# Token mixing with its tiles loaded into weight buffers, two batches in turn

## The chip, the cores and the metric

The kernel runs on one core of one Trainium2 chip. Its time is the device time in microseconds; three runs of the kernel before took 991.98 us (median), 991.78 and 993.13.

The core's engines each work through a queue of their own, in order: TensorE (PE in the rows, its weight loads PEld), VectorE (DVE), ScalarE (ACT), GpSimd (POOL) and SyncE (SP), which here only issues loads and stores. They wait for one another by semaphores.

## What is computed

Attention over 4 batches of 576 tokens and 8 heads, then two blocks over x of shape 4 x 576 x 512:

```python
def _moe_ref(x, w_ch1, w_ch2):                     # Fourier mixing and the first MLP
   X = np.fft.fft(np.fft.fft(x, axis=1), axis=2)
   u = x + np.real(X)
   un = (u - mu) / np.sqrt(var + 1e-06)            # mean and variance of a token
   return u + np.maximum(un @ w_ch1, 0.0) @ w_ch2  # 512 -> 2048 -> 512

def _moe2_ref(x, w_tok1, w_tok2, w_ch1, w_ch2):
   xt = x.transpose(0, 2, 1)
   h = np.maximum(xt @ w_tok1, 0.0) @ w_tok2       # token mixing: 576 -> 256 -> 576
   u = x + h.transpose(0, 2, 1)
   h2 = np.maximum(u @ w_ch1, 0.0) @ w_ch2         # second MLP: 512 -> 1536 -> 512
   return u + h2
```

## The kernel before

**Split numbers.** Every operand of these products is kept as a high and a low part (`hh` and `hl`, `ch` and `cl`, `uth` and `utl`, weights `..h` and `..l`), and each product is made three times: high by high, high by low, low by high. The weights of the block come in as doubles. `convert` (L73 to L85) loads 512 KB of them into `wraw` (three buffers), makes float32 of them in `wu` (two buffers), and takes the two parts: L78 on ScalarE, L80 on GpSimd, L81 to L83 on VectorE, L84 (high part) on ScalarE, L85 (low part) on GpSimd.

**Weight slots.** Four pools of 16 slots of 128 x 512 hold the weights: `wa`, `wx`, `wb` and `wc`. The first MLP's 16 steps f use four slots each (two matrices, two parts): f 0 to 3 in `wa`, 4 to 7 in `wx`, 8 to 11 in `wb`, 12 to 15 in `wc`. As its last chunk of tokens passes the steps, the slots come free, and `load_wb` fills them, one conversion a call: six for the token mixing (`wt1` and `wt2`, into `wa`), twelve `w1b` and twelve `w2b` of the second MLP. `w1b` go into `wa`, then `wx`, then `wb`; `w2b` into `wb` and, the last six, into the slots of `wa` that held `wt`.

**The MLPs.** The tokens stand in 18 tiles of 128, three tiles to a chunk, six chunks. In a step f of a chunk, `gemm1` makes 12 products of 384 columns (L346), ScalarE takes the relu as `hh` (L350), VectorE the rest `hl` (L351), and `gemm2` makes nine products of 512 columns (L364) into three accumulators that run over all f. The first MLP stores its result in `x2d`; the second takes its tiles from `u2d` (`u_load`), transposes them (L332, L335, L336), and stores the output.

**Token mixing.** Batch b has five tiles, the fifth with 64 rows. `c_load` loads them from `x2d` and splits them (high part on ScalarE, L566; low part on VectorE, L567). `c1(b)` makes 30 products (L614) into two accumulators, with the relu on ScalarE (L619) and its rest on VectorE (L620). `c2(b)` makes 30 more (L629), k over the two halves of the hidden tokens; VectorE adds each to the tile (L636), and SP stores it in `u2d` (L637). Even batches lie in buffers of the first MLP (`u`, `uth`, `utl`), odd ones in the pool `tok`, five buffers of each kind, which opens when `wc` is closed behind the first MLP. Batch 0's first three tiles are loaded in the last chunk of the first MLP, at f = 2; the rest behind it:

```python
        c_load(0, range(3, 5)); c_load(1, range(5)); load_wb()
        for b in range(B):
            hs = c1(b)
            load_wb()
            if b == 3:
                for i in range(2): m2.transposes(0, i, m2.u[0, i])
            c2(b, hs)
            if b + 2 < B: c_load(b + 2, range(5))
            if b == 2:
                for i in range(3): u_load(i)
            load_wb()
        m2.transposes(0, 2, m2.u[0, 2])
```

**What sets the order.** The code gives a program order, and a scheduler of the framework places the instructions of each engine in a queue from it; the slots of a pool are given out when the scheduler finds them free. Which instruction stands behind which is therefore read from the built program, below.

Of the kernel before, what the change touches and what calls it, by code (L numbers as in the profile page):

```python
# [18 lines left out]
DM = 512  # L19
P = 128  # L20
# [21 lines left out]
def attention_fourier_mlp_kernel(ctx: ExitStack, tc: tile.TileContext, a: dict, out: bass.AP):  # L42
# [28 lines left out]

# [1 line left out]
    def convert(src, hi, lo, n, eng):  # L73
# [18 lines left out]

# [1 line left out]
    lt = [(0, t) for t in range(6)]  # L94
# [121 lines left out]

# [1 line left out]
    class Fourier:  # L218
# [91 lines left out]

# [1 line left out]
    def spans(T):  # L312
# [90 lines left out]
    if True:  # L403
# [92 lines left out]

# [1 line left out]
        dp = dst.enter_context(tc.tile_pool(name="mlp", bufs=1, side="right", reuse_waits="tile"))  # L498
# [20 lines left out]
        def load_wb():  # L519
            engine[0] = nc.gpsimd  # L520
            if len(wt) < 12:
                nm, i = "12"[len(wt) // 6], len(wt) % 6 // 2
                src = a["wt" + nm]
                n = min(512, src.shape[1] // 2 - 512 * i)
                wt["h" + nm, i], wt["l" + nm, i] = slot_w(src[:, 1024 * i:1024 * i + 2 * n], wa, "wa", "wt", n)
            elif len(w1b) < NF2:
                f = len(w1b)
                pool, tag = (wa, "wa") if f < 2 else (wx, "wx") if f < 10 else (wb, "wb")
                w1b.append(slot_w(a["w1b"][f], pool, tag, "w1b"))
            elif len(w2b) < NF2:  # L530
                f = len(w2b)
                pool, tag = (wb, "wb") if f < 6 else (wa, "wa")
                w2b.append(slot_w(a["w2b"][f], pool, tag, "w2b"))
# [17 lines left out]
        def c_load(b, ts):  # L551
            for t in ts:
                p, j, (q0, n) = btiles(b)[t]
                if b % 2:
                    r = cp.tile([P, DM], F32, tag="cr", name="cr", bufs=5)
                    h = cp.tile([P, DM], F32R, tag="ch", name="ch", bufs=5)
                    l = cp.tile([P, DM], F32R, tag="cl", name="cl", bufs=5)
                else:
                    r = m1.u_tile(0)
                    if t % 3 == 0:  # L560
                        for nm in ("uth", "utl"):
                            xbuf[nm] = dp.tile([P, 3, DM], F32R, tag=nm, name=nm, bufs=2)
                    h, l = xbuf["uth"][:, t % 3], xbuf["utl"][:, t % 3]
                q = slice(q0, q0 + n)
                nc.sync.dma_start(out=r[q], in_=x2d[p][j, q, :])
                nc.scalar.activation(out=h[q], in_=r[q], func=AF.Copy)  # L566
                nc.vector.tensor_tensor(out=l[q], in0=r[q], in1=f32(h[q]), op=ALU.subtract)  # L567
                xs[b][t] = r, h, l
# [19 lines left out]
        def extra1(c, f):  # L588
            load_wa()
            if c == NCH - 1:  # L590
                if f >= 1:
                    load_wb()
                if f == 2:
                    c_load(0, range(3))

        steps = [(c, f) for h in range(len(PARTS) - 1) for c in range(2) for f in range(PARTS[h], PARTS[h + 1])]
        steps += [(c, f) for c in range(2, NCH) for f in range(NF1)]
        run(m1, steps, prep1, fin1, extra1)
        wcst.close()

# [1 line left out]
        cst = ExitStack()  # L602
        cp = cst.enter_context(tc.tile_pool(name="tok", bufs=1, side="left", reuse_waits="tile"))
        def c1(b):
# [11 lines left out]
            for m in range(2):  # L616
                hh = dp.tile([P, DM], F32R, tag="hh", name="hh", bufs=3)
                hl = dp.tile([P, DM], F32R, tag="hl", name="hl", bufs=3)
                nc.scalar.activation(out=hh, in_=hp[m], func=AF.Relu)  # L619
# [5 lines left out]
        def c2(b, hs):  # L625
# [6 lines left out]
            def fin(t, o):  # L632
# [3 lines left out]
                nc.vector.tensor_tensor(out=r[q], in0=o[q], in1=r[q], op=ALU.add)  # L636
                nc.sync.dma_start(out=u2d[p][j, q, :], in_=r[q])  # L637

# [19 lines left out]
        c_load(0, range(3, 5))  # L658
        c_load(1, range(5))
        load_wb()  # L660
        for b in range(B):
            hs = c1(b)
            load_wb()
            if b == 3:
                for i in range(2):
                    m2.transposes(0, i, m2.u[0, i])
            c2(b, hs)
            if b + 2 < B:
                c_load(b + 2, range(5))
            if b == 2:  # L670
                for i in range(3):
                    u_load(i)
            load_wb()
        m2.transposes(0, 2, m2.u[0, 2])
        cst.close()

# [1 line left out]
        def fin2(T, u):  # L678
# [16 lines left out]

        run(m2, [(c, f) for c in range(NCH) for f in range(NF2)], prep2, fin2, extra2)
        wbst.close()
        dst.close()


# [1 line left out]
PERM = np.concatenate([np.arange(288), np.arange(575, 287, -1)])  # L702
# [3 lines left out]

# [1 line left out]
def _split(x):  # L708
# [86 lines left out]
```

## Time and profile before

| | before |
|---|---|
| median of three runs | 991.98 us |
| span of the profiled execution, first to last instruction | 987.2 us |
| its end-to-end time | not given apart from the span |
| TensorE busy, share of the span | 949.3 us, 96% |
| VectorE busy | 472.8 us, 48% |
| ScalarE busy | 299.9 us, 30% |
| GpSimd busy | 236.1 us, 24% |
| share of the 16 DMA engines taken by SP's queue | 29.3% |
| moved by DMA | 93.00 MB |
| token mixing, first to last product of L614 and L629 | 595.2 to 676.6 us |
| its products, 120 of L614 and 120 of L629 | one of 512 columns: 0.39 to 0.40 us |

The span is on one clock for all engines. A product's own duration overlaps the next one's, so from one product to the next less time passes than the duration of one. The idle time that the profile gives for TensorE is therefore a little less than what is lost.

### The profile page before, as it was taken

The page shows a single profiled execution, that of the slowest core. Times are in us where ns is not written, and L with a number is a line of the kernel's source. Part 1 is how long each engine was busy: PE and PEld are TensorE (multiplying, and loading weights), DVE is VectorE, ACT ScalarE, POOL GpSimd, SP SyncE. Part 2 cuts the span into 40 slices and gives each one's busy share as a digit, 9 for nine tenths or more (in the row PEclk, how much of TensorE's full clock was granted, in tenths as well). Part 3 has the DMA queues.
Part 4 walks back from the last instruction along what each step waited for, and adds up shares of the span by engine and source line. Part 5 has one row for each costly group of instructions (what it writes and reads, how often), then busy time and mean ns, then how long its engine had stood idle before and what let it go on. Part 6 is the DMA issues. An engine that isn't in the chain of part 4 may idle for free.

```text
span 987.2 us, 13400 instructions
## 1 busy us (share of the span) xinstructions
PE 949.3 (96%) x5176; PEld 839.6 (85%) x5176; DVE 472.8 (48%) x895; ACT 299.9 (30%) x821; POOL 236.1 (24%) x187
## 2 busy tenths in 40 slices
PE   6988999999999999999999997989999999999998
PEld 6878888787889988999999995758998889998986
DVE  4679778999983412222123667884121212121211
ACT  5778664333431111111113334442111111111110
POOL 3466456443340000000002775643000000000000
PEclk9889999999999999999999998999999999999999
DMA  9997644243442100100102335682010201000100
GB/s 252 277 298 237 196 147 138 79 134 129 140 127 85 65 1 1 64 1 33 33 1 70 123 112 170 202 265 94 1 65 1 64 1 64 1 33 1 33 1 33
DMA packets 47215, 93.00 MB, mean 94 GB/s; under 512 B 5314, under 2 KB 15656, under 8 KB 47152
## 3 DMA queue, kind: packets, MB, share of 16 engines
q1 hardware_dynamic: 45184, 89.43, 29.3%
q0 software_dynamic: 1968, 2.72, 1.1%
q8 instruction: 41, 0.67, 0.3%
q14 instruction: 22, 0.18, 0.0%
HBM read 68.53 MB, written 23.60 MB: 93 GB/s over the span
## 4 chain that ended last, share of the span: by engine, by line
PE 62%; DVE 17%; DMA 9%; POOL 4%; issue 3%; ACT 3%; SPq 1%; DVEq 0%; POOLq 0%; ACTq 0%
PE oo L364 28%; PE h L346 28%; DVE wu L82 4%; DVE wu L83 3%; DMA xd<-x 2%; POOL wu L80 2%; DVE wu L81 2%; DMA cr<-x2d 1%; ACT sm L167 1%; PE ut L332 1%; DMA vs<-in_vs_dram 1%; PE av L190 1%; PE sc L149 1%; DVE xa L305 1%; DMA u<-ud 1%
## 5 line engine op out<-in xcount | busy, mean ns | idle before, releaser
L351 DVE SCALAR_TENSOR_TENSOR hl<-h,hh 128x384 fp32r<-128x384 f32 x168 | 93.0, 555 | 380.3 <-ACT hh L350 380.3
L350 ACT ACTIVATE hh<-h 128x384 fp32r<-128x384 f32 x168 | 81.9, 489 | 424.1 <-PE h L346 424.0
L346 PE MATMUL h<-uth,wAh 128*128 128x384 f32 x384 | 130.2, 340 | 0.0
L346 PE MATMUL h<-uth,wAl 128*128 128x384 f32 x384 | 129.6, 338 | 0.0
L346 PE MATMUL h<-utl,wAh 128*128 128x384 f32 x384 | 129.5, 337 | 0.0
L364 PE MATMUL oo<-wAh,hh 128*128 128x512 f32 x288 | 114.0, 398 | 1.5 <-DVE utl L336 0.9
L364 PE MATMUL oo<-wAl,hh 128*128 128x512 f32 x288 | 113.6, 394 | 0.0
L364 PE MATMUL oo<-wAh,hl 128*128 128x512 f32 x288 | 106.0, 395 | 2.4 <-DVE hl L351 2.4
L346 PE MATMUL h<-uth,w1bh 128*128 128x384 f32 x288 | 97.6, 340 | 0.0
L346 PE MATMUL h<-uth,w1bl 128*128 128x384 f32 x288 | 96.7, 336 | 0.0
L346 PE MATMUL h<-utl,w1bh 128*128 128x384 f32 x288 | 96.7, 336 | 0.0
L364 PE MATMUL oo<-w2bh,hh 128*128 128x512 f32 x216 | 86.1, 399 | 0.0
L364 PE MATMUL oo<-w2bl,hh 128*128 128x512 f32 x216 | 85.6, 396 | 0.0
L80 POOL TENSOR_SCALAR wu<-wu 128x512 f32<-128x512 f32 (+1 forms) x38 | 74.3, 1962 | 27.9 <-ACT wu L78 26.8
L364 PE MATMUL oo<-w2bh,hl 128*128 128x512 f32 x216 | 80.1, 394 | 0.0
L346 PEld LDWEIGHTS h<-uth,wAl 128*128 128x128 f32 x384 | 72.1, 188 | 3.2
L346 PEld LDWEIGHTS h<-utl,wAh 128*128 128x128 f32 x384 | 72.2, 188 | 2.5
L346 PEld LDWEIGHTS h<-uth,wAh 128*128 128x128 f32 x384 | 72.1, 188 | 1.9 <-issue 0.2
L167 ACT ACTIVATE sm<-sc,st 96x128 f32<-96x128 f32 (+2 forms) x176 | 61.4, 368 | 28.7 <-DVE st L165 22.4
L364 PEld LDWEIGHTS oo<-wAh,hl 128*128 128x128 f32 x288 | 53.9, 188 | 15.8 <-DVE hl L351 3.3
L85 POOL TENSOR_TENSOR wtl<-wu,wth 128x512 fp32r<-128x512 f32 (+1 forms) x6 | 6.9, 1149 | 242.3 <-ACT wth L84 242.3
L364 PEld LDWEIGHTS oo<-wAh,hh 128*128 128x128 f32 x288 | 54.1, 188 | 12.3 <-DVE u L368 1.4
(148 smaller groups left out, 1700.8 us busy)
## 6 DMA issues: line engine op xcount, KB each, us to landing
wraw<-in_w1a_dram SPq DMA_DIRECT2D x16, 512.0 KB
wraw<-in_w2a_dram SPq DMA_DIRECT2D x16, 512.0 KB
wraw<-in_w1b_dram SPq DMA_DIRECT2D x12, 512.0 KB
wraw<-in_w2b_dram SPq DMA_DIRECT2D x12, 512.0 KB
qz<-in_qt_dram SPq DMA_DIRECT2D x14, 288.0 KB
k<-in_kt_dram SPq DMA_DIRECT2D x7, 576.0 KB
vl<-in_vl_dram SPq DMA_DIRECT2D x4, 768.0 KB
x2d<-u SPq DMA_DIRECT2D x12, 256.0 KB
```

Of the source, the lines that this page charges most:

```text
L80: eng.tensor_scalar(f32(u), f32(u), E_MIN, E_MAX, op0=ALU.max, op1=ALU.min)
L81: v.tensor_scalar(u, u, 4, 1, op0=ALU.logical_shift_left, op1=ALU.logical_shift_right)
L82: v.scalar_tensor_tensor(out=u, in0=high, scalar=-2**31, in1=u, op0=ALU.bitwise_and, op1=ALU.bitwise_or)
L83: v.scalar_tensor_tensor(out=u, in0=low, scalar=29, in1=u, op0=ALU.logical_shift_right, op1=ALU.bitwise_or)
L149: nc.tensor.matmul(out=sc[:q, j * k:(j + 1) * k], lhsT=qz[self.g][:, hp, e, qs], rhs=k_t[self.b, self.g][:, hp, ks], start=False, stop=j = ...
L167: nc.scalar.activation(out=smv[:, j, :], in_=sc[:, j, :], func=AF.Exp, scale=SCALE, bias=st[:, 1, j:j + 1], accum_out=st[:, 2, j:j + 1])
L190: nc.tensor.matmul(out=self.o[:q, (2 * j + e) * 64:(2 * j + e + 1) * 64], lhsT=self.pt[e][:k, j * q:(j + 1) * q], rhs=v[:k, kv(t) if self. ...
L305: nc.vector.tensor_tensor(out=x[:n, 0:257], in0=x[:n, 0:257], in1=m[:n, 0:257], op=ALU.add)
L346: nc.tensor.matmul(out=h[:, :384], lhsT=l[:, ws], rhs=r[:, kd, :], start=x == 0, stop=x == 11)
L350: nc.scalar.activation(out=hh, in_=h[:, :384], func=AF.Relu)
L351: nc.vector.scalar_tensor_tensor(out=hl, in0=h[:, :384], scalar=0.0, in1=f32(hh), op0=ALU.max, op1=ALU.subtract)
L364: nc.tensor.matmul(out=self.o[c][i], lhsT=l[:, s], rhs=r, start=first and x == 0, stop=last and x == 2)
```

## The change

Batches 1 to 3 get slots of the weight pools: 1 and 3 in `wx`, 2 in `wc`; batch 0 stays where it was. The pool `tok` goes, and `wc` stays open to the end. Batch 1 is loaded in the last chunk of the first MLP at f = 9, batch 2 behind it, batch 3 after `c2(1)`. The second MLP's weights move to other pools accordingly. The products go as c1(0), c1(1), c2(0), c2(1), c1(2), c1(3), the transposes of the second MLP's first chunk, c2(2), c2(3). For this an odd batch's relu goes into `uth` and `utl` instead of `hh` and `hl`. The first three tiles of batch 0 are no longer stored in `u2d` and loaded again: the second MLP takes them where they lie.

```diff
-                pool, tag = (wa, "wa") if f < 2 else (wx, "wx") if f < 10 else (wb, "wb")
+                pool, tag = (wa, "wa") if f < 2 else (wb, "wb") if f < 10 else (wc, "wc")
                 w1b.append(slot_w(a["w1b"][f], pool, tag, "w1b"))
...
-                pool, tag = (wb, "wb") if f < 6 else (wa, "wa")
+                pool, tag = (wa, "wa") if f < 6 else (wc, "wc") if f < 9 else (wx, "wx")
                 w2b.append(slot_w(a["w2b"][f], pool, tag, "w2b"))
...
-                if b % 2:
-                    r = cp.tile([P, DM], F32, tag="cr", name="cr", bufs=5)
-                    h = cp.tile([P, DM], F32R, tag="ch", name="ch", bufs=5)
-                    l = cp.tile([P, DM], F32R, tag="cl", name="cl", bufs=5)
+                if b:
+                    pool, tag = (wc, "wc") if b == 2 else (wx, "wx")
+                    r = pool.tile([P, DM], F32, tag=tag, name="cr")
+                    h = pool.tile([P, DM], F32R, tag=tag, name="ch")
+                    l = pool.tile([P, DM], F32R, tag=tag, name="cl")
...
                 if f == 2:
                     c_load(0, range(3))
+                if f == 9:
+                    c_load(1, range(5))
...
-        wcst.close()
...
-        cst = ExitStack()
-        cp = cst.enter_context(tc.tile_pool(name="tok", bufs=1, side="left", reuse_waits="tile"))
         def c1(b):
...
-                hh = dp.tile([P, DM], F32R, tag="hh", name="hh", bufs=3)
-                hl = dp.tile([P, DM], F32R, tag="hl", name="hl", bufs=3)
+                if b % 2:
+                    if m == 0:
+                        th, tl = (dp.tile([P, 3, DM], F32R, tag=nm, name=nm, bufs=2) for nm in ("uth", "utl"))
+                    hh, hl = th[:, m], tl[:, m]
+                else:
+                    hh = dp.tile([P, DM], F32R, tag="hh", name="hh", bufs=3)
+                    hl = dp.tile([P, DM], F32R, tag="hl", name="hl", bufs=3)
...
-                nc.sync.dma_start(out=u2d[p][j, q, :], in_=r[q])
+                if b == 0 and t < 3:
+                    m2.u[0, t] = r
+                else:
+                    nc.sync.dma_start(out=u2d[p][j, q, :], in_=r[q])
...
-        c_load(1, range(5))
+        c_load(2, range(5))
+        hs = [c1(0), c1(1)]
         load_wb()
-        for b in range(B):
-            hs = c1(b)
+        for b in range(2):
+            c2(b, hs[b])
             load_wb()
...
+        c_load(3, range(5))
+        for b in range(2, 4):
+            hs.append(c1(b))
             load_wb()
-        m2.transposes(0, 2, m2.u[0, 2])
...
+        for i in range(3):
+            m2.transposes(0, i, m2.u[0, i])
+        for b in range(2, 4):
+            c2(b, hs[b])
+            for _ in range(2):
+                load_wb()
```

Three places in the queues show what the scheduler makes of it. The first is SP's queue around the end of the first MLP. `wraw` are raw weights, `x2d<-v` the stores of the first MLP's last three tiles, `cr<-x2d` loads of a batch of 1 to 3. Before, with batch 1's five loads among and behind those stores:

```order
L75 DMA wraw<-in_w1b_dram 128x1024 x12
L75 DMA wraw<-in_w2b_dram 128x1024 x3
L571 DMA x2d_78<-v 128x512
L565 DMA cr<-x2d_77 128x512
L571 DMA x2d_78<-v 128x512 x2
L565 DMA cr<-x2d_77 128x512 x3
L565 DMA cr<-x2d_77 64x512
```

Of the change, where batch 1's loads (`x2d_77`) stand a little further ahead among the `w1b`; these are the last of them, with batch 3's first, batch 2's five, and then the stores:

```order
L566 DMA cr<-x2d_77 64x512
L566 DMA cr<-x2d_78 128x512
L75 DMA wraw<-in_w1b_dram 128x1024 x4
L566 DMA cr<-x2d_78 128x512
L75 DMA wraw<-in_w1b_dram 128x1024
L566 DMA cr<-x2d_78 128x512
L75 DMA wraw<-in_w1b_dram 128x1024
L566 DMA cr<-x2d_78 128x512
L75 DMA wraw<-in_w2b_dram 128x1024
L566 DMA cr<-x2d_78 128x512
L566 DMA cr<-x2d_78 64x512
L75 DMA wraw<-in_w2b_dram 128x1024
```

Ten loads have moved ahead of the stores of the first MLP's last tiles.

The second place is TensorE's queue at the end of c1(0): `tk_5823` and `tk_5824` are its accumulators before, `hh_5855` its first relu, `tu` the accumulators of c2(0), `ch_5782` batch 1's first tile.

```order
L614 MATMUL tk_5824<-uth_5772,wth_5284 128x512
L614 MATMUL tk_5824<-utl_5773,wth_5284 128x512
L614 MATMUL tk_5824<-uth_5772,wtl_5285 128x512
L629 MATMUL tu_5875<-hh_5855,wth_5322 128x512
L629 MATMUL tu_5876<-hh_5855,wth_5322 128x512
L629 MATMUL tu_5877<-hh_5855,wth_5322 128x512
L614 MATMUL tk_5956<-ch_5782,wth_5194 128x512
```

Of the change, with `tk_5877` and `tk_5878` for c1(1) and `hh_5869` for the first relu of c1(0); fifteen products on `tk_5877` stand between c1(0) and the first of c2(0), and these are the last of them, with what follows:

```order
L614 MATMUL tk_5877<-cl_5544,wth_5232 128x512
L614 MATMUL tk_5877<-ch_5543,wtl_5233 128x512
L614 MATMUL tk_5877<-ch_5549,wth_5284 128x512
L614 MATMUL tk_5877<-cl_5550,wth_5284 128x512
L614 MATMUL tk_5877<-ch_5549,wtl_5285 128x512
L634 MATMUL tu_5927<-hh_5869,wth_5322 128x512
L634 MATMUL tu_5928<-hh_5869,wth_5322 128x512
L634 MATMUL tu_5929<-hh_5869,wth_5322 128x512
L614 MATMUL tk_5878<-ch_5525,wth_5194 128x512
```

Half of c1(1) has moved ahead of c2(0).

The third place is VectorE's queue at c2(2), whose additions are the rows of L636 before and of L641 now. Before, the five additions of batch 2 with the low parts of batch 3 among them:

```order
L636 TENSOR_TENSOR u_5920<-tu_6147,u_5920 128x512
L83 SCALAR_TENSOR_TENSOR wu_6405<-wraw_6403,wu_6405 128x512
L636 TENSOR_TENSOR u_5926<-tu_6148,u_5926 128x512
L636 TENSOR_TENSOR u_5930<-tu_6149,u_5930 128x512
L567 TENSOR_TENSOR cl_6073<-cr_6071,ch_6072 128x512
L567 TENSOR_TENSOR cl_6079<-cr_6077,ch_6078 64x512
L636 TENSOR_TENSOR u_5934<-tu_6174,u_5934 128x512
```

Of the change, from the last low part of batch 3 on; `wu_6242` is the third of `w2b`, `uth_6170` the second MLP's first chunk, `cr_5807` batch 2's first tile:

```order
L568 TENSOR_TENSOR cl_6064<-cr_6062,ch_6063 64x512
L641 TENSOR_TENSOR cr_5548<-tu_6017,cr_5548 64x512
L625 SCALAR_TENSOR_TENSOR utl_6153<-tk_6120,uth_6152 128x512
L336 TENSOR_TENSOR utl_6171<-ut_6172,uth_6170 128x4x128
L625 SCALAR_TENSOR_TENSOR utl_6153<-tk_6121,uth_6152 128x512
L81 TENSOR_SCALAR wu_6242<-wu_6242 128x512
L336 TENSOR_TENSOR utl_6171<-ut_6179,uth_6170 128x4x128
L82 SCALAR_TENSOR_TENSOR wu_6242<-wraw_6240,wu_6242 128x512
L641 TENSOR_TENSOR cr_5807<-tu_6193,cr_5807 128x512
L641 TENSOR_TENSOR cr_5813<-tu_6194,cr_5813 128x512
```

Batch 3's low parts have moved ahead of c2(2), and in their place two steps of a conversion stand in front of its first addition.

## Rows read from the trace of the kernel before

**Rows 1.** Windows: busy us of PE, PEld, DVE, ACT, POOL; PEclk, DMA share, GB/s.

```profile
610.00:620.00 10.00, 6.48 (x21) 5.21 (x22) 8.17 (x12) 4.72 (x8) 3.81 (x3) 0.66 0.57 203
660.00:670.00 10.00, 7.54 (x29) 5.22 (x29) 5.85 (x8) 4.68 (x8) 6.92 (x5) 0.83 0.83 273
```

**Rows 2.** Waits of TensorE from 590 to 700 us.

```profile
PE tk L614 <- ACT ch L566: 5.5, 2, 4.0
PE ut L332 <- DMA u<-u2d: 2.5, 2, 2.2
PE tu L629 <- ACT hh L619: 1.5, 1, 1.5
PE tu L629 <- DVE u L636: 0.5, 1, 0.5
```

**Rows 3.** Timeline of TensorE: start us, duration, product, idle time before it.

```profile
602.18 0.39 PE L364 MATMUL oo<-wAh,hl 128*128 128x512 f32 x1
602.41 0.40 PE L614 MATMUL tk<-utl,wth 128*128 128x512 f32 x1
...
606.72 0.39 PE L614 MATMUL tk<-uth,wtl 64*128 64x512 f32 x1
608.58 0.96 PE L629 MATMUL tu<-hh,wth 128*128 128x512 f32 x3 [1.47 <-ACT hh L619]
613.52 0.79 PE L614 MATMUL tk<-ch,wth 128*128 128x512 f32 x1 [3.98 <-ACT ch L566]
...
617.00 0.86 PE L629 MATMUL tu<-hh,wth 128*128 128x512 f32 x3
...
645.13 0.39 PE L629 MATMUL tu<-hh,wtl 128*128 128x512 f32 x1
647.08 0.73 PE L614 MATMUL tk<-ch,wth 128*128 128x512 f32 x2 [1.57 <-ACT ch L566]
...
661.42 0.39 PE L614 MATMUL tk<-ch,wtl 64*128 64x512 f32 x1
663.99 0.66 PE L332 MATMUL ut<-ident_r,u 128*128 128x128 f32 x4 [2.18 <-DMA u<-u2d]
...
668.20 0.40 PE L629 MATMUL tu<-hh,wtl 128*128 128x512 f32 x1
...
678.42 0.40 PE L364 MATMUL oo<-w2bh,hh 128*128 128x512 f32 x1
```

**Rows 4.** Chain that ended last, 635 to 655 us: start us, us, what.

```profile
639.52 4.06 DMA u2d<-cr
...
645.16 6.39 DMA cr<-x2d
```

**Rows 5.** L567 by its line, and L80 on the page: durations in ns.

```profile
L567 DVE TENSOR_TENSOR utl<-u,uth x10: 674/683/1099, 529.3 to 636.3; 128x512 fp32r<-128x512 f32 x8, 64x512 fp32r<-64x512 f32 x2
L567 DVE TENSOR_TENSOR cl<-cr,ch x10: 677/690/693, 613.5 to 658.4; 128x512 fp32r<-128x512 f32 x8, 64x512 fp32r<-64x512 f32 x2
...
L80 POOL TENSOR_SCALAR wu<-wu 128x512 f32<-128x512 f32 (+1 forms) x38 | 74.3, 1962 | 27.9 <-ACT wu L78 26.8
```

**Rows 6.** Timeline of ScalarE: first and last high part of w2b, two relus.

```profile
616.22 0.61 ACT L84 ACTIVATE w2bh<-wu 128x512 fp32r<-128x512 f32 x1
...
682.46 0.63 ACT L84 ACTIVATE w2bh<-wu 128x512 fp32r<-128x512 f32 x1 [2.70 <-DVE wu L83]
...
686.99 0.49 ACT L350 ACTIVATE hh<-h 128x384 fp32r<-128x384 f32 x1 [3.52 <-PE h L346]
691.23 0.49 ACT L350 ACTIVATE hh<-h 128x384 fp32r<-128x384 f32 x1 [3.75 <-PE h L346]
```

**Rows 7.** Timeline of SP and VectorE in a quiet stretch of the first MLP.

```profile
315.03 1.51 SPq L571 DMA_DIRECT2D x2d<-u  x3
317.10 1.01 SPq L380 DMA_DIRECT2D u<-ud  x2
...
319.75 1.53 DVE L389 BATCH_NORM_STATS2 bs<-u 128x6 f32<-128x512 f32 x2 [1.81 <-DMA u<-ud]
```

More of the change, by code (lines that the diff above doesn't have):

```diff
@@ L658, in attention_fourier_mlp_kernel @@
         c_load(0, range(3, 5))
-        c_load(1, range(5))
+        c_load(2, range(5))
+        hs = [c1(0), c1(1)]
         load_wb()
-        for b in range(B):
-            hs = c1(b)
+        for b in range(2):
+            c2(b, hs[b])
             load_wb()
[L664 to L672, printed above, removed]
-            load_wb()
-        m2.transposes(0, 2, m2.u[0, 2])
-        cst.close()
+        c_load(3, range(5))
+        for b in range(2, 4):
+            hs.append(c1(b))
+            load_wb()
+        for i in range(3):
[4 more added lines that the diff above has]
+                load_wb()
         def fin2(T, u):
@@ L696, in attention_fourier_mlp_kernel @@
         run(m2, [(c, f) for c in range(NCH) for f in range(NF2)], prep2, fin2, extra2)
+        wcst.close()
         wbst.close()
```

## The prediction

> **What bounds the kernel now.** The profile's first two parts and then the windows were read first: TensorE is busy in nearly all of the span (the table above), and the one stretch after the attention in which it is not is the token mixing, some 80 us long. There the windows show 6.48 and 7.54 us of products in ten, and a granted clock of 0.66 and 0.83 on the mean, where 1.00 is the upper of TensorE's two levels (2.4 GHz) and 0.50 the lower (1.2): the lower one for two thirds and one third of those windows [rows 1]. On both sides the products stand end to end, so any time that TensorE gets back here comes off the end of the kernel: the chain of waits from here on is products alone. The view of TensorE's waits for this stretch then says on whom it waits: ScalarE's copies of batch 1's and 3's tiles, twice, 5.5 us; the loads of the second MLP's first tiles, 2.5 us; once on a relu and once on an addition, 2.0 us [rows 2].
>
> The size of each is best read from product to product in the timeline, since the ends of products are modelled. Two neighbours start 0.23 us apart (602.18 and 602.41, where the first MLP ends) [rows 3]. What lies above that [rows 3]:
> - 606.72 to 608.58, c2(0) waits for the relu of c1(0), which it follows directly: 1.86 - 0.23 = 1.63 us.
> - 608.58 to 613.52, three products and then batch 1's first tile: 4.94 - 0.69 = 4.25 us.
> - 613.52 to 617.00, eight products at the lower clock: 3.48 - 1.84 = 1.64 us.
> - 645.13 to 647.08, batch 3's first tile: 1.95 - 0.23 = 1.72 us.
> - an accumulator that VectorE has not emptied: 0.5 us [rows 2].
> - 661.42 to 663.99, the first tiles of the second MLP come back from memory: 2.57 - 0.23 = 2.34 us.
> - 663.99 to 668.20, at the lower clock again: six products (1.38) and eight transposes. A transpose moves a quarter of a product's columns; estimated at 0.09 us, between a quarter and a half of a product's step, they make 0.7. Lost: 4.21 - 1.38 - 0.7 = 2.13 us.
>
> The sum is 14.2 us. That is the most that this stage can give back, but for small change where products of 64 and 128 rows follow each other, which both kernels have.
>
> Why are the tiles late? Batch 1 has buffers of its own in a pool that opens when the last weights of the first MLP are free, and its loads stand in SP's queue behind the store of the first MLP's last tiles. Batch 3 takes batch 1's buffers, so its load waits 4.06 us for a store and then takes 6.39 [rows 4].
>
> **The change, part by part.** *Batch 1 into wx, batch 2 into wc, both while the first MLP still runs.* SP's rows show batch 1's five loads and the first of batch 3 among the w1b loads, batch 2's behind them, all ahead of the store that they stood behind. The 4.25 and, with it, the 1.64 at the lower clock go. The copies and low parts (ten L567 of 0.69 us, 6.9 us in all on VectorE [rows 5]) move from the token mixing under the last ten steps of the first MLP, of 4.24 us each [rows 6]: 0.69 more in a step that TensorE fills with products. I cost that at nothing; if the cover is gone, it costs what the third and fourth rival say. What the weights pay for the slots comes under w2b below.
>
> *Both products over two batches in turn.* TensorE's rows show c1(1) between c1(0) and c2(0), so fifteen products, 3.5 us, stand where TensorE waited 1.63 for the relu: that goes. The number of products, copies, additions and conversions is the same.
>
> *Batch 3 over batch 1's slots.* This wait stays in kind: the low part of its fourth tile stands in VectorE's queue until the store of batch 1's first tile has landed, behind it the addition of batch 1's second tile, whose store lets the load of batch 3's last tile go, and then its copy. Allowed is the time from the last product of batch 1's first tile to the first product on batch 3's last tile: by TensorE's rows 62 products and three transposes, with the row changes between 64 and 128 rows some 15.3 us. Needed, in a quiet time: a store lands in 2.07 us (315.03 to 317.10, where a load waits for it) and a load in 2.65 (317.10 to 319.75, its reader) [rows 7]: 1.7 until the first addition has gone through VectorE, 2.07, 0.69 low part, 0.68 addition, 2.07, 2.65, 0.63 copy: 10.5 us, no wait. In the busiest: 1.7 + 4.06 + 1.37 + 4.06 + 6.39 + 0.63 = 18.2, a wait of 2.9 [rows 4]. Only two raw loads are let go in that time, and both before the second store, so I take the quiet end, 0.
>
> *The conversions of w2b wait longer.* Before, the first w2b was converted at 616.22 [rows 6]; now its slots are those of wt1, and its place in ScalarE's queue is behind batch 3's last copy. Ahead of it GpSimd's queue stands still as well: the eleventh w1b takes slots in wc that batch 2's first tile lets go only in c1(2), some 75 products, 18 us, behind the first MLP. VectorE's rows show where this is felt: L81 and L82 of the third w2b stand ahead of c2(2)'s additions, and the next accumulators of c2 wait for these. Nothing shows the size of that wait in the new order; its kind is there once now with 0.5 us [rows 2]. Below it could be nothing, above it could cost twice the 1.72 of a late tile, 3.4. I take two of the known size, 1.0 us, since two conversion steps stand ahead.
>
> *The second MLP's first tiles stay.* Three stores and three loads of 256 KB go, and the 2.34 and 2.13 us with them: the transposes take tiles that VectorE finished in c2(0), with c2(1), c1(2) and most of c1(3) between.
>
> Sum: 14.2 - 1.0 = 13.2 us. The span is 987.2 us, and the median of the runs is 4.8 above it; the profiled execution's own end-to-end time isn't given apart, so these 4.8 us are taken as what lies around. 991.98 - 13.2 = 978.8 us.
>
> **A rule against it.** The ten L567 now run while GpSimd converts weights. The row: twenty of them took 0.67 to 1.10 us with a median of 0.68 and 0.69 [rows 5], while GpSimd was busy 3.81 and 6.92 us of ten [rows 1]; so they are hardly held up. The Trainium skill (SBUF — State Buffer, Who interferes with whom) says that a VectorE instruction with two SBUF inputs contends with a GpSimd instruction that reads SBUF, and that the later one blocks until the other is through. By that rule each could be held for one GpSimd step, and the sum would be that of the fourth rival.
>
> **Rivals.**
> 1. *The wait moves to batch 3's last tile.* For it: VectorE and SP stand one behind the other through two stores and a load. 2.9 us, and the two gaps above 2 us were each followed by products at the lower clock, so 2.1 more: 983.8 us. Against: the raw loads are through by then.
> 2. *Slower: the second MLP waits for w2b.* Before, nine of twelve were converted when its products began, now about three. The first conversion ends some 0.6 us behind the first product on batch 3's last tile: 602.4 plus 162 products, three transposes and the row changes, 642.5. The twelfth is needed eleven steps behind the first product on w2b: 678.42 - 13.2 [rows 3] + 11 x 4.24 = 711.9. At the pace of before, (682.46 - 616.22) / 11 = 6.02 us [rows 6], it is there at 708.7. From 6.3 us each on, TensorE waits, eleven times the excess; from 7.5 on, the gain is gone, and at 8 the time is 978.8 + 11 x 1.7 = 997.5 us. Against: the 6.02 itself holds waits for slots, which are free sooner now.
> 3. *Relus late in the first MLP.* ScalarE takes them in turn with the copies of batch 1 and 2, which wait for their loads. A slot is let go one step, 4.24 us, ahead of its copy; a load beside raw weights takes 6.39 [rows 4]: 2.15 late, five tiles of batch 2: 10.8. A relu has some products ahead of it, and I have no row for how many microseconds that is: half, 5.4: 984.2 us.
> 4. *VectorE held up by GpSimd.* Ten times one L80 of 1.96 us [rows 5] is 19.6 on VectorE; half of it at TensorE: 988.6 us. Against: the medians.
>
> **Chances and range.** My forecast 0.62, between 977.8 (no new wait) and 981.2 (3.4 us of it); rival 1 0.13, rival 2 0.12, of which 0.03 end near no change, rival 3 0.08, rival 4 0.05. What a measurement here can tell from no change is about 0.2%, 2 us. Faster by more than that: 0.62 + 0.13 + 0.08 + 0.05 = 0.88; the same 0.03; slower 0.09. The range takes in rivals 1 and 3 and leaves 2 and 4 out (0.17): 977.0 to 985.5, its lower end 0.8 below the case without any new wait, for what the sum's steps of 0.23 may be off.
>
> **What would show it.** Right: no wait of TensorE for a copy of cr or for u2d in its first chunk; a granted clock of 1.00 throughout this stage; c2(0) without a gap; short waits on VectorE's additions around c2(2). Wrong: a wait ahead of batch 3's last tile; idle TensorE in the last chunk of the first MLP, with ScalarE waiting for cr; products on w2b that wait for L84 or L85.

## The result, and the profile after

The change took 983.09 us (median of 4 runs, 981.91 to 984.13) against 991.88 before (4 runs, 987.72 to 993.13), a ratio of 0.990 with an interval of 0.986 to 0.994. A second set of runs gave 982.28 (6 runs) against 992.23 (17 runs, 987.41 to 999.17), 0.9895 (0.9856 to 0.9934). The forecast was 978.8, with 977.0 to 985.5 as its range.

The two windows of [rows 1], now of the change:

```profile
610.00:620.00 10.00, 10.00 (x40) 6.63 (x39) 7.96 (x13) 3.52 (x7) 1.53 (x1) 1.00 0.62 189
660.00:670.00 10.00, 10.00 (x49) 8.51 (x48) 7.50 (x13) 2.12 (x4) 3.14 (x3) 1.00 0.86 258
```

TensorE has no idle time there any more, and its clock is the upper one throughout. GpSimd, which converts weights, is busy 1.53 us of ten instead of 3.81; the stage begins 7.5 us later in this trace, and in the first ten us behind the first MLP's last product it is 1.80 instead of 6.94. Keep these numbers in mind. Of TensorE's waits from 520 to 700 us only one is left, and it is not in the token mixing but in the last chunk of the first MLP:

```profile
PE oo L364 <- DVE hl L351: 1.2, 1, 1.2
```

TensorE's timeline shows the stage as [rows 3] did:

```profile
521.13 0.60 PE L332 MATMUL ut<-ident_r,lm 128*128 128x128 f32 x4
...
609.73 0.39 PE L364 MATMUL oo<-wAh,hl 128*128 128x512 f32 x1
609.96 0.39 PE L614 MATMUL tk<-utl,wth 128*128 128x512 f32 x1
...
614.59 0.50 PE L614 MATMUL tk<-ch,wth 128*128 128x512 f32 x1
...
618.48 0.96 PE L634 MATMUL tu<-hh,wth 128*128 128x512 f32 x3
...
650.55 0.73 PE L614 MATMUL tk<-ch,wth 64*128 64x512 f32 x2
...
673.55 0.40 PE L364 MATMUL oo<-w2bh,hh 128*128 128x512 f32 x1
...
975.13 0.84 PE L364 MATMUL oo<-w2bh,hl 128*128 128x512 f32 x3
```

From here on two stretches are compared, each the difference of two such rows. **A** goes from the first MLP's last transposes to its last product, 521.13 to 609.73: the last chunk, 88.60 us. **B** goes from there to the last product of all, 609.73 to 975.13: 365.40 us. Before, with 602.18 from [rows 3] and these two, A is 87.11 and B 981.49 - 602.18 = 379.31.

```profile
515.07 0.60 PE L332 MATMUL ut<-ident_r,lm 128*128 128x128 f32 x4
...
981.49 0.86 PE L364 MATMUL oo<-w2bh,hl 128*128 128x512 f32 x3
```

So B is 13.9 us shorter, and A 1.5 longer. Ahead of A, where both kernels have the same queues, this execution of the change happened to be 6.1 us later (521.13 against 515.07).

### The profile page after: what moved, and what is told of

It reads as the page before. It is cut to its first block, busy times and chain, and to the rows that moved or that the text cites. A ratio compares the mean times of both kernels' runs of the same rounds, so it can differ in the third digit from the quotient of the medians.

```text
span 980.6 us, 13395 instructions
## 1 busy us (share of the span) xinstructions
PE 948.8 (97%) x5176; PEld 840.1 (86%) x5176; DVE 471.6 (48%) x895; ACT 300.0 (31%) x821; POOL 235.6 (24%) x187
## 4 chain that ended last, share of the span: by engine, by line
PE 75%; DVE 13%; DMA 6%; issue 2%; ACT 2%; SPq 1%; POOL 0%; DVEq 0%; POOLq 0%
PE oo L364 32%; PE h L346 31%; PE tk L614 3%; PE tu L634 3%; DMA xd<-x 3%; DVE wu L82 3%; PE sc L149 1%; DVE wu L83 1%; PE av L190 1%; ACT sm L167 1%; PE ut L332 1%; DMA vs<-in_vs_dram 1%; DVE xa L305 1%; DMA u<-ud 1%; DVE u L368 1%
## 5 line engine op out<-in xcount | busy, mean ns | idle before, releaser
L80 POOL TENSOR_SCALAR wu<-wu 128x512 f32<-128x512 f32 (+1 forms) x38 | 74.8, 1975 | 28.5 <-ACT wu L78 24.5
L85 POOL TENSOR_TENSOR wtl<-wu,wth 128x512 fp32r<-128x512 f32 (+1 forms) x6 | 6.8, 1148 | 242.5 <-ACT wth L84 242.5
```

Source lines behind the costliest of these rows:

```text
L80: eng.tensor_scalar(f32(u), f32(u), E_MIN, E_MAX, op0=ALU.max, op1=ALU.min)
```

## The experiments

Twelve kernels were run. The table has the whole of what they showed; below they stand by what they ask.

| run | time, us | ratio to before (interval) | A | B |
|---|---|---|---|---|
| before, its first trace | 991.88 | | 87.11 | 379.31 |
| again_before | 993.09 | 1.0008 (0.9979 to 1.0037) | 87.10 | 378.41 |
| change, its first trace | 983.09 | 0.990 (0.9863 to 0.9938) | 88.60 | 365.40 |
| again_after | 982.28 | 0.9895 (0.9856 to 0.9934) | 88.32 | 365.40 |
| loads_alone | 981.71 | 0.9875 (0.983 to 0.9921) | 87.88 | 365.62 |
| batch1_late | 980.56 | 0.9883 (0.9841 to 0.9925) | 87.11 | 365.52 |
| both_late | 978.69 | 0.9853 (0.9802 to 0.9905) | 87.10 | 363.99 |
| slots_alone | 981.71 | 0.9886 (0.9808 to 0.9964) | 87.10 | 366.49 |
| before_hold | 986.01 | 0.9933 (0.9902 to 0.9964) | 87.11 | 372.74 |
| before_hold2 | 985.41 | 0.9934 (0.9904 to 0.9963) | 87.10 | 369.77 |
| early1_running | 988.32 | 0.9958 (0.993 to 0.9986) | 88.73 | 371.90 |
| early1_held | 984.16 | 0.9894 (0.9844 to 0.9943) | 88.39 | 366.22 |
| rows64_together | 981.42 | 0.9874 (0.9832 to 0.9917) | 88.93 | 364.66 |
| loads_ahead | 983.47 | 0.9897 (0.9857 to 0.9937) | 87.14 | 364.68 |

**again_before, again_after**: the two kernels as they are, for second traces.

> The kernel before, unchanged, for a second trace. The first trace of the change lost 4.0 us against that of before ahead of the first MLP (its first product at 167.88 against 163.86 us), though the queues are the same up to there. If this is a difference from one execution to the next, this trace or its times show it without the change: a first product near 168 us and a span near 990, and several of the runs near 992 us with others near 988. If the change itself slows the attention, the first product stands at 163.9 us again and the times within 0.2% of one another.

> The changed kernel, unchanged. From the first MLP's last product to the eighth step of the second MLP the first traces took 106.1 us before and 92.5 now: 13.6 us less. If the rest of the difference (6.6 us of span instead of 13.6) is variation of the executions ahead of it, the ratio of the times comes to 0.987 to 0.990 over more runs, and the wait of 1.2 us for VectorE's low part in the first MLP's last chunk, behind batch 1's last copy, is there again. If that wait is chance, it is gone in this trace.

The first MLP's first product stood at 168.67 us in this trace of before and at 166.46 in this one of the change, so the 4.0 us ahead of it were not the change's. Its place went from 163.86 to 173.79 us over all the traces, with equal queues up to there. A and B on the other hand repeat better: B was 365.40 in both traces of the change, and 0.9 us apart in those of before. The wait in A was there again (0.90 instead of 1.18 us), so it is no accident. From here on A and B decide, since a difference of 1 us can't be read from the times. Each of the other kernels has one trace.

**loads_alone**: batches 1 to 3 in weight slots, the rest undone.

```diff
-        hs = [c1(0), c1(1)]
...
+        for b in range(4):
+            hs = c1(b)
...
+            if b == 3:
+                for i in range(3):
+                    u_load(i)
+                for i in range(3):
+                    m2.transposes(0, i, m2.u[0, i])
+            c2(b, hs)
...
```

> Batches 1 to 3 in weight slots as in the change, but the products written batch by batch, and the first three tiles stored and loaded again. Theory A, the prediction's sum: the order is worth 1.6 us and the first tiles in place 4.5 (2.34 of wait and 2.13 at the lower clock), so this is 6.1 us slower than the change, 989 us. Theory B, the early tiles do nearly all: with them there the scheduler puts half of c1(1) ahead of c2(0) by itself, and the tiles of the second MLP are loaded in time: within 1.5 us of the change, 982 to 985 us, no wait of TensorE above 0.5 us for a relu or for a load.

B was 365.62 and TensorE waited for nothing from 600 to 700 us. Theory A was wrong: with the tiles in weight slots, the written order and the tiles in place are worth 0.2 us together. The scheduler puts fifteen products of c1(1) ahead of c2(0) by itself, and the three tiles come back from memory in time.

**batch1_late**, then **both_late**: the change, with tiles that can't be early: batch 1, and then batch 2 too, reads the rows of the first MLP's last three tiles, and so waits for their stores. These kernels compute the batch from other tokens, and their output is not the block's; the number of loads, products and slots is the same.

```diff
-                nc.sync.dma_start(out=r[q], in_=x2d[p][j, q, :])
+                src = x2d[1][6 + t % 3, q, :] if b == 1 else x2d[p][j, q, :]
+                nc.sync.dma_start(out=r[q], in_=src)
...
-                if f == 9:
-                    c_load(1, range(5))
...
+        c_load(1, range(5))
         c_load(2, range(5))
```

In both_late the condition is `b in (1, 2)`.

> The change, but batch 1 reads the rows of the first MLP's last three tiles, so that its loads wait for their stores (batch 1 is computed from other tokens); order, slots and the tiles in place stay. Theory A, the early load of batch 1 carries 4.25 + 1.64 us: c2(0) stands behind c1(0) again and waits 1.6 for the relu, c1(1) waits 0 to 4 us for its tiles and the clock falls: 985 to 990 us. Theory B, the two batches in turn hide a late tile: less than 1 us slower than the change.

> The run before with batch 2 made late as well: batches 1 and 2 read the rows of the first MLP's last three tiles (both are computed from other tokens), so no tile but batch 0's is there when the first MLP ends; slots, order and the tiles in place stay as in the change. Theory A, one batch that is there early is what the scheduler fills the stage with: now TensorE waits for copies again, 4 to 8 us in all with the time at the lower clock, and the stretch from the first MLP's last product to the last product, 365.4 us in the change and 365.5 with batch 1 late, grows to 370 to 373. Theory B, it isn't the early load but that the w2b conversions stand still here, which leaves ScalarE, GpSimd and the queues to batch 1 and 2: at most 2 us of waits, 365.5 to 367.5.

B was 365.52 and 363.99, with at most one wait of 0.2 us. So the early load, which the prediction had as the main thing, can be taken away, for one batch and for both, and nothing is lost; A even falls to 87.1, as before the change. That brought up theory B: what matters is that the conversions stand still here.

**before_hold**: the kernel before with the two halves of w2b exchanged, so that the first six wait for `wt`.

```diff
-                pool, tag = (wb, "wb") if f < 6 else (wa, "wa")
+                pool, tag = (wa, "wa") if f < 6 else (wb, "wb")
```

> The kernel before with the two halves of w2b exchanged: the first six take the slots of wt, the last six those of wb, so the conversions stand still through most of the token mixing as they do in the change; loads, order and first tiles are those of before. Theory A (early tiles): the waits for batch 1's and 3's copies and for u2d stay, 8 to 11 us above the products' steps between the first MLP's last product and the first w1b product. Theory B (conversions out of the way): the relu of c1(0) is no longer late (1.6 us gone), and batch 1's loads, without raw weights beside them, land 1 to 2 us earlier: 4 to 6 us left. In both the second MLP's first chunk may wait for w2b, up to 20 us, since the conversions begin only behind c1(3); that part says nothing on this question.

Neither was right as it stood. B fell by 5.7 to 6.6 us, to 372.74, from two numbers in one line. But what went were the later waits (batch 3's copy, u2d and the lower clock behind them); the first two stayed whole, 1.69 and 4.23 us. At that time it was the last two w1b that were converted, not w2b.

**slots_alone**: loads_alone with both batches late, as in both_late. **before_hold2**: the last two w1b are held as well, and w2b behind them, since the conversions go in order; the diff is that of before_hold2.

```diff
-                pool, tag = (wa, "wa") if f < 2 else (wx, "wx") if f < 10 else (wb, "wb")
+                pool, tag = (wx, "wx") if 2 <= f < 10 else (wa, "wa")
...
-                pool, tag = (wb, "wb") if f < 6 else (wa, "wa")
+                pool, tag = (wb, "wb") if f < 8 else (wa, "wa")
```

> The weight slots of the change and nothing else of it: products written batch by batch, the first three tiles through memory, and batches 1 and 2 read the rows of the first MLP's last three tiles (both are computed from other tokens), so that neither is there early. Theory A: two batches in turn and the tiles in place carried the stage while both batches were late; without them the waits for copies and for u2d come back, 5 to 10 us, and the stretch from the first MLP's last product to the last product is 370 to 375 us. Theory B: the slots are what counts, since they hold the conversions back until the third batch is under way: 364 to 366.5 us, at most 2 us of waits.

> The kernel before with the last two w1b in the slots of wt1, so that all conversions from w1b's eleventh on stand still from the end of the first MLP until c1(3) is through; loads, buffers, order and first tiles are those of before. Holding w2b alone removed the later waits of the stage, not the first two (1.69 and 4.23 us and the lower clock behind them). Theory B (conversions in the way of ScalarE's relu and VectorE's last additions of the first MLP, on which the stores and batch 1's loads wait): now these shrink too, to at most 2.5 us together. Theory A (batch 1's own late load, behind the stores in SP's queue): 4 to 6 us of them stay. The second MLP may wait for weights in its first chunk, which is read apart.

Slots alone, with no tile early, no order and nothing in place, gave 366.49: 1.1 us short of the whole change, and 2.5 short of both_late, which has late tiles too, but the order and the tiles in place. The windows of slots_alone show GpSimd without any work at the time at which it was busy before [rows 1]:

```profile
610.00:620.00 10.00, 10.00 (x42) 7.60 (x42) 5.92 (x10) 3.72 (x6) 0.00 (x0) 1.00 0.75 264
620.00:630.00 10.00, 9.57 (x43) 6.38 (x41) 4.52 (x7) 3.16 (x5) 0.00 (x0) 1.00 0.98 320
```

The kernel before with its conversions held came to 369.77. The wait for the relu is gone there, and of the stage's waits one is left:

```profile
PE tk L614 <- ACT ch L566: 2.9, 1, 2.9
```

How the conversions were in the way is read from the timeline of the kernel before, ScalarE's rows at the end of the first MLP:

```profile
605.34 0.63 ACT L84 ACTIVATE w1bh<-wu 128x512 fp32r<-128x512 f32 x1 [2.12 <-DVE wu L83]
605.88 0.66 ACT L78 ACTIVATE wu<-wraw 128x512 f32<-128x512 f32 x1
606.44 0.63 ACT L566 ACTIVATE uth<-u 128x512 fp32r<-128x512 f32 x1
607.37 0.67 ACT L78 ACTIVATE wu<-wraw 128x512 f32<-128x512 f32 x1 [0.30 <-POOL w1bl L85]
607.95 0.57 ACT L619 ACTIVATE hh<-tk 128x512 fp32r<-128x512 f32 x1
612.84 0.63 ACT L566 ACTIVATE ch<-cr 128x512 fp32r<-128x512 f32 x1 [4.31 <-DMA cr<-x2d]
```

The relu at 607.95 stands behind a conversion's L84 that waited 2.12 us for VectorE and an L78 that waited for GpSimd. In slots_alone ScalarE sat idle 7.60 us ahead of the same relu, ready for it:

```profile
601.83 0.68 ACT L78 ACTIVATE wu<-wraw 128x512 f32<-128x512 f32 x1
610.11 0.60 ACT L623 ACTIVATE hh<-tk 128x512 fp32r<-128x512 f32 x1 [7.60 <-PE tk L613]
```

There the relu starts 3.2 us behind the first MLP's last product (606.92); before, 5.8 us behind it (602.18). VectorE's queue had conversions in it as well. Before, L83 stood ahead of the first MLP's last additions (L368), behind whose stores batch 1's loads stand, so that these additions began 3.1 us behind the last product:

```profile
603.65 1.66 DVE L83 SCALAR_TENSOR_TENSOR wu<-wraw,wu 128x512 int32<-128x512 int32 x1
605.23 1.87 DVE L368 TENSOR_TENSOR v<-oo,v 128x512 f32<-128x512 f32 x3
```

In slots_alone the last two began 0.5 us behind it:

```profile
607.39 1.28 DVE L368 TENSOR_TENSOR v<-oo,v 128x512 f32<-128x512 f32 x2
```

Why the conversions stand still is in the slots: the eleventh w1b needs those that batch 2 holds until c1(2), and w2b those of wt1.

Held conversions are not all that the slots do for late batches: with these held in both, before_hold2 is 3.3 us longer than slots_alone. Its trace differs in two things. The last steps of the tenth w1b still stand ahead of L368, which begins 2.1 us behind the last product. And the scheduler puts nine products of c2(0) ahead of batch 1's first one (three before, eighteen in slots_alone), so that this one meets its late copy:

```profile
615.95 0.85 PE L614 MATMUL tk<-ch,wth 128*128 128x512 f32 x2 [2.88 <-ACT ch L566]
```

In slots_alone the copy has come when TensorE gets there:

```profile
616.10 0.86 PE L613 MATMUL tk<-ch,wth 128*128 128x512 f32 x3
```

No run takes these two apart.

**early1_running, early1_held**: does an early batch 1 help when the conversions run on? Batches 1 and 3 go into `wx` in the kernel before, and w1b and w2b where slots are free; in the second, the last two w1b and the last four w2b go into `wa` again.

```diff
-                pool, tag = (wa, "wa") if f < 2 else (wx, "wx") if f < 10 else (wb, "wb")
+                pool, tag = (wa, "wa") if f < 2 else (wb, "wb") if f < 10 else (wc, "wc")
...
-                pool, tag = (wb, "wb") if f < 6 else (wa, "wa")
+                pool, tag = (wc, "wc") if f < 6 else (wa, "wa")
...
-                    r = cp.tile([P, DM], F32, tag="cr", name="cr", bufs=5)
+                    r = wx.tile([P, DM], F32, tag="wx", name="cr")
...
```

> The kernel before, with batches 1 and 3 in slots of wx so that batch 1 comes in under the first MLP; w1b and w2b go to wb and wc, where slots are free, so the conversions run on through the stage as they do before. Batch 2's buffers, the written order and the first tiles are those of before. The stretch from the first MLP's last product to the last product is 378.4 to 379.3 us before, 365.4 in the change, 366.5 with the slots alone and both batches late, 369.8 before with the conversions held. If an early batch 1 is enough by itself, the first two waits go although the conversions run (the scheduler puts half of c1(1) behind c1(0)): 368 to 371 us, the waits for batch 3 and for u2d staying or going with it. If the conversions are what delays this stage, at least 4 us of waits are left in all: 373 to 378 us.

> The run before this, with the last two w1b in the slots of wt1, so that the conversions stand still from the first MLP's end until c1(3) is through, as in the second run on the kernel before. With that one (369.8 us, batch 1 late) and the run before this it makes two by two: batch 1 early or late, conversions running or held. If the two causes add up, this one loses nothing more in the stage: 365.0 to 366.5 us. If one of them is enough, it is within 1 us of the better of the other two.

It does. Early means here the load and the order that the scheduler makes of it, with half of c1(1) ahead of c2(0). B in us, two by two:

| | conversions run on | conversions held |
|---|---|---|
| batch 1 late | 378.4, 379.3 | 369.8 |
| batch 1 early | 371.9 | 366.2 |

Holding is worth 8.6 to 9.5 us with a late batch 1 and 5.7 with an early one; an early load 6.5 to 7.4 and 3.6. Each removes half of the loss or more, and the two together, less than their sum, nearly all of it. The waits that stay when the conversions run on are of the kind that [rows 2] show:

```profile
PE tk L610 <- ACT ch L566: 1.4, 1, 1.4
PE tu L625 <- ACT hh L615: 0.7, 1, 0.7
PE tu L625 <- DVE cr L632: 0.5, 1, 0.5
PE tk L610 <- ACT uth L566: 0.3, 1, 0.3
```

**rows64_together**, then **loads_ahead**: what the change still leaves.

```diff
-            for ts in ((0, 1, 2), (3, 4)):
+            for ts in ((0, 1, 2), (3,), (4,)):
```

The second adds that a tile of batch 1 is allocated and loaded one tile ahead:

```diff
             for t in ts:
...
+                for s in (t, t + 1):
+                    if s in ts and s not in lead and (s == t or b == 1):
+                        load(s)
```

> The change, with the products on 64 rows of both halves of c1 one behind the other. In the change's trace, products about a change between 128 and 64 rows lose 0.09 to 0.11 us each, eight of them in c1(0), 0.82 us. If it is the change of rows that costs this, half of the changes in c1 go, and with four batches the stretch from the first MLP's last product to the last product shrinks from 365.4 to 363.8 to 364.2. If it is something else about these products (their weight loads, the accumulator), it stays within 0.3 us of 365.4.

> The run before this, and batch 1's tiles loaded one tile ahead of their copies' slots. In the change, the copy of batch 1's last tile waits for its load in ScalarE's queue, behind it a conversion's first step, GpSimd's, VectorE's and at last the low part that TensorE waits for: 1.2 and 0.9 us in the two traces of the change, 0.45 in that of the loads alone, none where batch 1 came late. If that chain is the cause, the wait in the first MLP's last chunk goes to below 0.3 us; if the early conversions themselves are too slow for a step of 4.2 us, it stays at 0.4 to 1.2. Time 979 to 981 us against 982.3 for the change, which the spread of the runs may cover.

With the 64-row products of c1(0) side by side, c1(0) took 4.25 us from the first product behind the first MLP to the first of batch 1 (610.32 to 614.57) instead of 4.63 (609.96 to 614.59 in the change). The scheduler let only two of the four batches be written so (seven stretches of 64-row products are left of nine), hence 0.74 us in B instead of 1.2 to 1.6. In loads_ahead the wait in A is gone and A is back at 87.14. This is the best of the kernels that compute the whole: A + B is 451.8 us, against 454.0 and 453.7 in the traces of the change. The times don't show it (983.47): the spread ahead of the first MLP covers it, whose first product stood at 173.79 us in this trace.

## Why the prediction was right, and where not

**The size of the stage's loss: right.** The sum said that 14.2 us could come back and 13.2 would. B gave back 13.0 (378.41 - 365.40) to 13.9.

**Its cause: half of it.** The first step that failed is "*The conversions of w2b wait longer*", which was priced at -1.0 us, with a bound of -3.4. What was seen of it was right (GpSimd's queue stands still until c1(2)), and the sign was wrong: the standstill cleared ScalarE's and VectorE's queues and, in the kernel before, was worth 5.7 us beside an early batch 1 and 9 without. There was no wait for an addition around c2(2). The terms 4.25 and 1.64 were given to batch 1's early load alone. It does take them away, but so do the slots with late loads (slots_alone); held conversions by themselves leave 3.04 and 1.58 of them (before_hold2).

**"I cost that at nothing": wrong.** The copies and low parts under the first MLP cost 1.2 to 1.5 us in A; the chain is told under rival 3. The wait for additions that didn't come had been priced at 1.0, so the two errors nearly cancel in the time: that part of the hit is luck.

**"c2(0) waits for the relu of c1(0), which it follows directly": wrong.** c2(0)'s first products need the relu of c1(0)'s first half only, and six products lie between. The relu was late because ScalarE's queue had conversions in front of it. With these held and the order of before, the wait is gone (before_hold2). So it was no matter of the order, and two batches in turn were worth nothing once the slots and the early tiles were there (loads_alone). With late tiles, order and tiles in place together gave 2.5 us (both_late against slots_alone).

**The first tiles in place, 2.34 + 2.13: not theirs.** before_hold (conversions held) and early1_running (conversions on, batch 1 early) both lost this wait with the tiles still going through memory.

**Batch 3's last tile: right.** Forecast quiet, 10.5 us of 15.3 allowed. Measured the same way it was 12.8 of 16.1: its product came at 650.55 without a wait, 3.3 us after its copy ended.

**w2b for the second MLP: right.** The first high part was written at 647.99 and the last at 703.11, 5.0 us each, and no product on w2b waited. Rival 2 had its point at 7.5 us each.

```profile
647.99 0.64 ACT L84 ACTIVATE w2bh<-wu 128x512 fp32r<-128x512 f32 x1 [0.74 <-PE tk L614]
...
703.11 0.63 ACT L84 ACTIVATE w2bh<-wu 128x512 fp32r<-128x512 f32 x1 [2.54 <-DVE wu L83]
```

**Rival 3 came true beside the forecast**, with 1.2 to 1.5 us of its 5.4. In the change, ScalarE's rows in the last chunk of the first MLP are:

```profile
577.43 0.63 ACT L567 ACTIVATE ch<-cr 64x512 fp32r<-64x512 f32 x1 [4.04 <-DMA cr<-x2d]
578.08 0.68 ACT L78 ACTIVATE wu<-wraw 128x512 f32<-128x512 f32 x1
578.65 0.63 ACT L84 ACTIVATE w1bh<-wu 128x512 fp32r<-128x512 f32 x1
579.18 0.49 ACT L350 ACTIVATE hh<-h 128x384 fp32r<-128x384 f32 x1
```

The relu at 579.18 is in time all the same. What is late is its low part on VectorE: that stands behind L81 of the conversion whose L78 stood behind the waiting copy, with GpSimd's L80 between.

```profile
580.80 1.50 DVE L81 TENSOR_SCALAR wu<-wu 128x512 int32<-128x512 int32 x1 [2.02 <-POOL wu L80]
582.22 0.54 DVE L351 SCALAR_TENSOR_TENSOR hl<-h,hh 128x384 fp32r<-128x384 f32 x1
```

TensorE then goes on at 582.82, having waited 1.18 us. Some 1.07 of this is the 1.50 us of L81 above its median of 0.43, an estimate; the last section has the reason. Late batches (A = 87.10 or 87.11 in seven traces, before's two among them) or a load one tile ahead (87.14, the copy waits 1.28 us instead of 4.04) take it away: this chain is shown.

**The 4.8 us "around" the span were a misreading**, though nothing in the sum hangs on it, which takes 13.2 off the median. The time lies 1.7 to 2.1 us above the span in every run since. So the profiled execution of before, with its span of 987.2, took about 989.0 us: it stood in the lower part of before's runs and was set beside the median of others. The forecast was 3.5 to 4.3 us too low. From A and B the change is worth 12.1 us (the mean of 466.4 and 465.5 less that of 454.0 and 453.7), so 980 from the 992.2 of before; what is measured above that, 2 to 3 us, lies within the spread of the stretch ahead of the first MLP, whose cause stays open.

Not tried: early tiles for batches 1 and 2 while the conversions run on, since the four pools have no place for them: two batches take 30 of the 64 slots, wt 12, and the 22 that are left hold eleven w1b at most.

Why both_late is 1.4 us better than the change in B can be read from its trace. It has six stretches of 64-row products where the change has nine, and in one of them those of batch 1 (rows 64 to 127) and batch 2 (rows 0 to 63) stand side by side. Seven products start there within 0.70 us, 0.12 apart instead of 0.23:

```profile
630.40 0.40 PE L613 MATMUL tk<-cl,wth 64*128 64x512 f32 x1
630.41 0.50 PE L613 MATMUL tk<-ch,wth 64*128 64x512 f32 x1
630.64 0.39 PE L613 MATMUL tk<-ch,wtl 64*128 64x512 f32 x1
630.75 0.51 PE L613 MATMUL tk<-cl,wth 64*128 64x512 f32 x2
630.98 0.51 PE L613 MATMUL tk<-ch,wtl 64*128 64x512 f32 x2
```

Three stretches at 0.37 us (0.74 for two in rows64_together) and 0.7 us here, less 0.3 for its one wait, make 1.5: an estimate, and no run isolates it.

## What to carry to other kernels

A wait names the last releaser; look at what stood in front of that releaser in its own queue before giving the time to an edit. Background work (here weight conversions) in the queues of a short critical stage can cost more than late loads, and a pool's slots decide when it runs: one or two of the lines that choose a pool gave 5.7 to 9.5 us of the stage. Undo each part of a change by itself: of three edits here one carried nearly all of it, in part for a reason that was counted as its price. And compare stretches of the trace that repeat to within 1 us, where the times of whole runs spread by 5 to 14.

## What the runs showed of the hardware

L81, a VectorE step with one input, took a median of 0.43 us over its 62 instances in the change, and 1.50 in the row above; it started 0.07 us after a GpSimd step and ended 0.29 us after that one:

```profile
580.73 1.28 POOL L85 TENSOR_TENSOR w1bl<-wu,w1bh 128x512 fp32r<-128x512 f32 x1
```

It is no single case: in each of the fourteen traces, an L81 that began more than 0.1 us before the end of such an L85 ended 0.28 to 0.29 us behind that end, whether it had begun 0.04 or 0.9 us behind the start of the L85. The Trainium skill (SBUF — State Buffer, Who interferes with whom) says that a tensor_scalar can run in a mode that takes the port pair which VectorE shares with GpSimd, and that the one that issues later then waits until the other is through: these rows agree with the wait; that L81 runs in this mode they can't show.

The prediction had looked for it at the wrong GpSimd step. The subtraction with two inputs, which by the same section contends too, kept its median (0.69 us over 15 instances in the change, the longest 1.10). But twelve of these subtractions, over all traces, began more than 0.1 us before the end of an L85, and each ended 0.55 us behind that end, after 0.69 to 1.38 us. Of 58 that began beside an L80, which has one input, 41 kept 0.67 to 0.70 us and 17 took about 1.1. So beside an L85 the later step waits for the end; beside an L80, from which the fourth rival took its price of 1.96 us each, it mostly does not.

In TensorE's timeline the first product behind a change from 128 to 64 rows, or back, starts 0.32 to 0.33 us after its predecessor, and the next 0.33 to 0.34 later, where 0.23 is the rule. In the change:

```profile
611.59 0.40 PE L614 MATMUL tk<-uth,wtl 128*128 128x512 f32 x1
611.92 0.50 PE L614 MATMUL tk<-uth,wth 64*128 64x512 f32 x1
612.26 0.39 PE L614 MATMUL tk<-utl,wth 64*128 64x512 f32 x1
612.49 0.39 PE L614 MATMUL tk<-uth,wtl 64*128 64x512 f32 x1
612.81 0.50 PE L614 MATMUL tk<-uth,wth 128*128 128x512 f32 x1
613.15 0.39 PE L614 MATMUL tk<-utl,wth 128*128 128x512 f32 x1
```

rows64_together, where two of c1(0)'s four changes were saved with the products the same, shows that it is the changes that cost it: 0.38 us for two. A change from 128 to 64 columns, or back, costs nothing: in the change there are four, at 0.23 to 0.24 us.

```profile
631.71 0.40 PE L634 MATMUL tu<-hh,wtl 128*128 128x512 f32 x1
631.94 0.39 PE L634 MATMUL tu<-hh,wth 128*64 128x512 f32 x1
```

The Trainium skill (TensorEngine Tiling (Array Packing), Key Properties) says that a change of the tiling mode drains TensorE; the rows agree for a change of rows, and give its price. For a change of columns they show no such cost.
